# One NeuronCore, adaLN + S4 convolution + squared-ReLU FFN: the first inverse stage in two 64-column tiles, and a re-planned order of the instructions

## The chip, the cores and the metric

The kernel runs on one core of a Trainium2 chip. The metric is the device time of one execution in microseconds (us); lower is better. Each kernel is timed several times, and one further execution is taken with the hardware profiler; all rows of the profile are of that one execution.

## The reference

Input `A_u` has 2048 positions of 512 channels, all float32.

```python
sa, ca, ga, sb, cb, gb = six rows of silu(c) @ w_mod
h = layernorm(x) * (1 + ca) + sa
x = x + ga * ssm_conv(h)              # per channel
h = layernorm(x) * (1 + cb) + sb
x = x + gb * (relu(h @ w1 + b1) ** 2 @ w2 + b2)
# ssm_conv: K[d, l] = Re sum_n C[d,n] dB[d,n] exp(dt A[d,n] l)   (128 states n)
#           y = causal convolution of h with K along l (FFTs of length 4096 in the reference) + h * Dskip
```

The result has the shape of the input.

## The kernel before

**Convolution.** The 512 channels are cut into 8 chunks of 64 (`NC`), and each chunk into 4 units of 16 channels, 32 units in all. The convolution is done with a Fourier transform written as matmuls. For each chunk these pieces exist on PE:

- kernel generation, one per unit ("K", `kgen_mm`, L751): 32 matmuls of 32-column tiles that sum the 128 states into the convolution kernel of 16 channels, in the PSUM bank `kg`;
- stage 1 (`stage1`, L615): 8 matmuls per piece, 64-column stationary tiles; 4 pieces for the input `u` and 4 for the kernel, copied out by ACT (L617);
- stage 2 (`stage2`, L625): 16 matmuls per piece, 64-column tiles, again 4 pieces for each of the two; the result of `u` is copied by ACT (L650) and, once complete, swapped half for half into a second buffer by a DMA on the SP queue (L654); the result of the kernel is multiplied on DVE (L761) with `u` and its swapped copy;
- first inverse stage ("E", L769): 4 pieces of 8 matmuls with 128-column stationary tiles, copied out by ACT (L773).

**What feeds K.** For each chunk POOL makes phase tables with nine integer additions (L684) and scales the amplitudes (L706), and ACT makes 24 exponentials (L703). For each unit POOL adds up the phases (L712, 128x1024) and makes three products of amplitudes (L734, 128x512, two or three named `rtl` and one `rtl` or `llph`); ACT takes sine, absolute value and cosine (L721 to L723); DVE multiplies them together (L740 to L744). The products live in rings of three, so POOL can be three units ahead of K. Once, at the start, `parameters` derives what the tables need from the inputs, on DVE, ACT and POOL (L443 to L493): first for chunk 0 alone, later for chunks 1 to 7 together (128x448 elements, written 7x64). `scale` normalizes the input of a chunk with three DVE instructions of 128x1024 (L603 to L605) and one on POOL (L606).

**After the convolution** the second inverse stage (`inverse`, L937, 32x32 tiles) adds up the result, and the FFN follows (L1031 to L1034 and L1051 to L1053), with its weights split into two parts by ACT (L887, L883) and POOL (L908, L884).

**The order of the work.** Python writes the pieces down in one sequence: `background` gives each chunk's `u` pieces and product pieces a place (`u0` to `u1`, counted in units) between the units. This sequence settles which buffers of the rings a piece uses. Then `keep_order` decides the order on each engine: it walks through all instructions with a price for each (`weight`), starts on the engine that is free first, and picks among the ready instructions the one with the longest priced path to the end, plus a bonus in ns from `urgent` (set by `hurry`). Every engine then executes that list strictly in order. DVE instructions that share a memory port with POOL (`shares_port`) get an extra price.

Of the kernel before, what the change touches and what calls it, by code (L numbers as in the profile page):

```python
# [36 lines left out]
NC = 512 // NCH  # L37
# [58 lines left out]
def weight(ins):  # L96
# [3 lines left out]
    if "DMA" in type(ins).__name__:  # L100
# [12 lines left out]
            tiles = 128 // cols if cols in (32, 64, 128) else 1  # L113
            t = 2.2 * max(moving / 1.2 / tiles + 2, {128: 112, 64: 28}.get(cols, 13))
            return t, t + 170
        case "Activation":
            t = 75 + 0.87 * n + (40 if n > 512 else 0)
            if n == 1:
                t = 200
# [6 lines left out]
            if n <= 4:  # L126
                t = 200
        case "Pool":
            t = 110 + 1.8 * n
        case _:  # L130
# [4 lines left out]
def keep_order(tc, traced, slots, in_turn, whole, urgent):  # L135
# [85 lines left out]
    for g, n in enumerate(left):  # L221
        if n == 0:
            ready[of[g][0]].append(g)
    landed = table = 0
    WINDOW = 3413
# [9 lines left out]
    for _ in groups:  # L235
# [6 lines left out]
        cost = takes[g][0]  # L242
        if e == "PE":
            cost /= level(now)
            a = now
            while a < now + cost - 1:
# [3 lines left out]
                a = b  # L250
        elif e == "DVE" and shares_port(groups[g][0]):
            cost += min(650, max(0, free["Pool"] - now))
        elif e == "Activation":
            new = function_table(groups[g][0]) or table
            cost += 1283 if new != table else 0
            table = new
# [20 lines left out]
def tile_adaln_ssm_ffn(  # L277
# [244 lines left out]
    for i, t in enumerate((mean, rstd)):  # L522
        nc.vector.tensor_copy(t.rearrange("p (s g) -> p s g", g=4), moved[:, :, :, i])
    hurry(mark, 60000)

    for _ in parameters(1, NC - 1):
        pass

# [8 lines left out]
    def mod_rows(wm, ps):  # L537
        for q in range(4):
            for kc in range(4):
                nc.tensor.matmul(  # L540
# [214 lines left out]
    def product_pieces(c):  # L755
# [9 lines left out]
        for g in range(4):  # L765
            ps = bank("ps", PS)
            for i in range(4):
                for h, y in ((0, yu), (1, yr)):
                    nc.tensor.matmul(  # L769
                        ps[:, 128 * i : 128 * i + 128], pairs(y)[:, g, i // 2, :, i % 2],  # L770
                        e1_sb[:, h], start=(h == 0), stop=(h == 1))
            for r in range(2):
# [21 lines left out]
    def background():  # L794

        parts = [(late, 4, 5, 1)]
        for c in range(NC):
            u0 = max(4 * c, 3.9) + (2 if c == 1 else 0)
            parts.append((lambda c=c: u_pieces(c), u0, u0 + (2 if c < 2 else 2.6), 9))
        for c in range(NC - 1):  # L800
            u0 = 4 * c + (4 if c > 0 else 6)
            parts.append((lambda c=c: product_pieces(c), u0, u0 + (2.5 if c == 0 else 3), 8))
        todo = sorted(
# [321 lines left out]
```

## Time and profile before

| what | value |
|---|---|
| median of 3 runs | 712.5 us (709.61 to 714.19) |
| the profiled execution itself | 709.58 us |
| span shown in its profile | 707.8 us |
| PE busy | 596.5 us, 84% of the span |
| DVE, ACT, POOL busy | 392.0, 380.0, 345.3 us |
| first K, unit 0 | starts at 63.05 us |
| last K, unit 31 | starts at 332.05 us |
| second inverse stage | starts at 357.47 us |

Times in rows of the profile are from the start of the span. A row of the timeline gives start, length, engine, line, operation, output<-input, shape and count, and in brackets how long the engine stood idle before and what ended that. PE is the matmuls, PEld the loads of stationary tiles. One float32 matmul of the program leaves two records on PE, so a piece of stage 1 (8 matmuls) is "x16", a piece of stage 2 or a K "x32" or "x64". Lengths of PE rows overlap by some 0.1 us; the price of a piece is best read from one start to the next.

### The profile page before, as it was taken

The page shows a single profiled execution, that of the slowest core. Times are in us where ns is not written, and L with a number is a line of the kernel's source. Part 1 is how long each engine was busy: PE and PEld are TensorE (multiplying, and loading weights), DVE is VectorE, ACT ScalarE, POOL GpSimd, SP SyncE. Part 2 cuts the span into 40 slices and gives each one's busy share as a digit, 9 for nine tenths or more (in the row PEclk, how much of TensorE's full clock was granted, in tenths as well). Part 3 has the DMA queues.
Part 4 walks back from the last instruction along what each step waited for, and adds up shares of the span by engine and source line. Part 5 has one row for each costly group of instructions (what it writes and reads, how often), then busy time and mean ns, then how long its engine had stood idle before and what let it go on. Part 6 is the DMA issues. An engine that isn't in the chain of part 4 may idle for free.

```text
span 707.8 us, 18955 instructions
## 1 busy us (share of the span) xinstructions
PE 596.5 (84%) x8306; PEld 516.4 (73%) x8306; DVE 392.0 (55%) x622; ACT 380.0 (54%) x760; POOL 345.3 (49%) x316
## 2 busy tenths in 40 slices
PE   1321695766989999999868999999999999999996
PEld 1311584765989889999846788888888888888884
DVE  5788889975677576861245784243332533252233
ACT  3464867555999999875626464223432334222220
POOL 5768999999798798740969571000100000000000
PEclk9855798888999999999977999999999999999998
DMA  9990002020202022353822220001000100010001
GB/s 328 374 362 10 3 2 63 1 61 2 63 4 63 18 48 62 106 132 82 288 89 63 77 74 1 1 0 60 0 1 1 60 1 1 0 46 15 1 1 59
DMA packets 22274, 46.38 MB, mean 66 GB/s; under 512 B 3760, under 2 KB 9264, under 8 KB 20400
## 3 DMA queue, kind: packets, MB, share of 16 engines
q1 hardware_dynamic: 21760, 45.04, 20.4%
q8 instruction: 65, 1.06, 0.6%
q10 hardware_dynamic: 432, 0.14, 0.1%
q14 instruction: 17, 0.14, 0.1%
HBM read 32.58 MB, written 4.19 MB: 52 GB/s over the span
## 4 chain that ended last, share of the span: by engine, by line
PE 63%; POOL 20%; DMA 5%; DVE 5%; ACT 5%; issue 3%; DVEq 0%; SPq 0%; POOLq 0%; ACTq 0%
PE tg L1051 7%; PE tg L1053 7%; PE tg L1052 7%; PE ps L769 6%; PE ps L1031 6%; PE ps L1032 6%; PE ps L1034 5%; POOL rtl L734 5%; POOL tables L684 5%; PE ps L625 5%; POOL llph L712 4%; PE ps L615 3%; PE tg L937 2%; PE kg L751 2%; DMA xy<-xt 2%
## 5 line engine op out<-in xcount | busy, mean ns | idle before, releaser
L1039 DVE TENSOR_TENSOR xy<-xy 128x512 f32<-128x512 f32 x56 | 43.9, 784 | 158.9 <-ACT rw L1038 107.6
L1037 ACT ACTIVATE xy<-ps,b1c 128x512 f32<-128x512 f32 x42 | 29.0, 690 | 130.7 <-PE ps L1034 130.7
L966 POOL TENSOR_TENSOR big<-big,b2g 128x512 f32<-128x512 f32 x16 | 21.1, 1318 | 157.7 <-DVE xy L964 153.4
L734 POOL TENSOR_TENSOR rtl<-tables 128x512 f32<-128x512 f32 x75 | 83.9, 1142 | 8.7 <-issue 5.7
L625 PE MATMUL ps<-xy,t_sb 128*64 128x64 f32 x2048 | 71.0, 228 | 10.8 <-DVE xy L761 6.6
L769 PE MATMUL ps<-e_sb,xy 128*128 128x128 f32 x512 | 70.9, 296 | 8.4 <-ACT big L773 5.5
L625 PEld LDWEIGHTS ps<-xy,t_sb 128*64 128x64 f32 x2048 | 67.0, 143 | 14.1 <-DVE xy L761 6.9
L769 PEld LDWEIGHTS ps<-e_sb,xy 128*128 128x128 f32 x512 | 65.5, 204 | 12.0 <-ACT big L773 5.9
L712 POOL TENSOR_TENSOR llph<-tables 128x1024 int32<-128x1024 int32 x32 | 65.1, 2034 | 15.5 <-ACT tg L723 15.3
L617 ACT COPY xy<-ps 128x512 f32<-128x512 f32 x64 | 36.7, 590 | 18.9 <-PE ps L615 18.4
L743 DVE TENSOR_TENSOR rtl<-rtl,tg 128x1024 f32<-128x1024 f32 x32 | 38.9, 1217 | 14.2 <-ACT tg L723 13.4
L721 ACT ACTIVATE tg<-llph 128x1024 f32<-128x1024 int32 x32 | 33.1, 1034 | 25.0 <-POOL llph L712 20.4
L761 DVE TENSOR_TENSOR xy<-ps,xy 128x512 f32<-128x512 f32 x64 | 39.7, 681 | 7.1 <-DMA xy<-xy 6.3
L615 PE MATMUL ps<-d_sb,ksb 128*64 128x128 f32 x512 | 34.2, 281 | 7.1 <-ACT xy L617 4.2
L773 ACT COPY big<-ps 128x256 f32<-128x256 f32 x64 | 33.9, 626 | 10.4 <-PE ps L769 10.4
L615 PE MATMUL ps<-d_sb,big 128*64 128x128 f32 x512 | 33.7, 280 | 5.2 <-DVE xy L761 4.5
L723 ACT ACTIVATE tg<-llph,halfpi 128x1024 f32<-128x1024 f32 x32 | 36.0, 1126 | 1.5 <-DVE llph L744 0.9
L1031 PE MATMUL ps<-h0h,w1h 128*128 128x512 f32 x88 | 36.1, 410 | 0.0
L740 DVE SCALAR_TENSOR_TENSOR rtl<-rtl,tg 128x512 f32<-128x512 f32 x32 | 21.8, 681 | 25.4 <-ACT tg L721 12.4
L540 PE MATMUL ps<-xy,srep 128*32 128x128 f32 x192 | 19.7, 353 | 18.9 <-DMA xy<-w_mod 13.6
L615 PEld LDWEIGHTS ps<-d_sb,ksb 128*64 128x64 f32 x512 | 28.5, 140 | 9.3 <-ACT xy L617 4.7
L722 ACT ACTIVATE llph<-llph 128x1024 f32<-128x1024 int32 x32 | 34.0, 1062 | 0.3
(236 smaller groups left out, 1546.5 us busy)
## 6 DMA issues: line engine op xcount, KB each, us to landing
xy<-xt SPq DMA_DIRECT2D x32, 256.0 KB, 5.4
xy<-xy SPq DMA_DIRECT2D x16, 512.0 KB, 5.9
xy<-w_mod SPq DMA_DIRECT2D x6, 1024.0 KB, 12.4
big<-x SPq DMA_DIRECT2D x4, 1024.0 KB, 11.9
out_dram<-xy SPq DMA_DIRECT2D x16, 256.0 KB, 2.1
xy<-w SPq DMA_DIRECT2D x14, 256.0 KB, 2.8
raw<-w SPq DMA_DIRECT2D x6, 512.0 KB, 5.5
t_sb<-c_t SPq DMA_DIRECT2D x1, 2048.0 KB, 17.1
```

The costliest lines, as they stand in the source:

```text
L615: nc.tensor.matmul(ps[64 * r : 64 * r + 64, 128 * i : 128 * i + 128], src[:, i], d1_sb[:, r], start=True, stop=True)
L625: nc.tensor.matmul(ps[64 * r : 64 * r + 64, 64 * i : 64 * i + 64].rearrange("p (h q t) -> p q h t", h=2, t=2), t2_sb[:, 8 * g + i, r], src ...
L712: nc.gpsimd.tensor_tensor(ph.rearrange("p d r (a b) -> p (d r) a b", a=4), bc(lo[:, us].rearrange("p d r b -> p (d r) b"), 2, 4), bc(hi[:, ...
L734: nc.gpsimd.tensor_mul(o.rearrange("p d (a b) -> p d a b", a=4), bc(p, 3, 8), bc(q, 2, 4))
L761: nc.vector.tensor_mul(product_piece(y, g), ps, piece(x, g))
L769: nc.tensor.matmul(ps[:, 128 * i : 128 * i + 128], pairs(y)[:, g, i // 2, :, i % 2], e1_sb[:, h], start=(h == 0), stop=(h == 1))
L1031: pe.append(nc.tensor.matmul(ps, w1h[:, q, fs], hh[:, q, :], start=(q == 0), stop=False))
L1032: pe.append(nc.tensor.matmul(ps, wl[:, q], hh[:, q, :], start=False, stop=False))
L1039: nc.vector.tensor_mul(rr, rr, rr)
L1051: pe.append(nc.tensor.matmul(acc, r2l[:, ms], hi_, start=(t == 0), stop=False))
L1052: pe.append(nc.tensor.matmul(acc, r2h[:, ms], lo_, start=False, stop=False))
L1053: pe.append(nc.tensor.matmul(acc, r2h[:, ms], hi_, start=False, stop=(t == NF - 1)))
```

## The change

It has three parts.

**E in two tiles.** Each matmul of the first inverse stage, which had a stationary tile of 128 columns, becomes two with 64 columns each that write the two halves of the output partitions. 256 matmuls become 512; the moving operand is the same for both.

**Prices of the planner.** In `weight` the prices of PE shapes, of the reciprocal, of very small DVE instructions and of POOL are replaced; `keep_order` adds 100 ns where PE's shape changes and treats the shared port of DVE and POOL in both directions. No instruction is added or left out by this; only the order moves.

**Places.** The pieces of the chunks get places from two tables. The parameters of chunks 1 to 7 get the bonus of 60000 ns that the statistics of the first layer norm (L508 to L524) had, and these get none. In `mod_rows` the loops are exchanged, so that neighbouring matmuls go to different 32-column tiles.

```diff
-            t = 2.2 * max(moving / 1.2 / tiles + 2, {128: 112, 64: 28}.get(cols, 13))
+            t = max(1.7 * moving / tiles, 60 / tiles)
...
             if n <= 4:
-                t = 200
+                t = 150
+            elif type(ins).__name__ == "InstReciprocal":
+                t = 70 + 6.3 * n
         case "Pool":
-            t = 110 + 1.8 * n
+            t = 180 + 1.72 * n
...
+            kind = free_size(groups[g][0].ins[1]) if len(groups[g][0].ins) > 1 else shape
+            cost += 100 if kind != shape else 0
+            shape = kind
...
-        elif e == "DVE" and shares_port(groups[g][0]):
-            cost += min(650, max(0, free["Pool"] - now))
+        elif e == "DVE":
+            port = shares_port(groups[g][0])
+            cost += min(700, max(0, free["Pool"] - now)) if port else 0
+        elif e == "Pool":
+            cost += min(250, max(0, free["DVE"] - now)) if port else 0
...
-    hurry(mark, 60000)
-
-    for _ in parameters(1, NC - 1):
-        pass
+    hurry(mark, 0)
+
+    for c, n in ((1, 7),):
+        mark = len(nc.cur_bb.bb.instructions)
+        for _ in parameters(c, n):
+            pass
+        hurry(mark, 60000)
...
-        for q in range(4):
-            for kc in range(4):
+        for kc in range(4):
+            for q in range(4):
...
-                    nc.tensor.matmul(
-                        ps[:, 128 * i : 128 * i + 128], pairs(y)[:, g, i // 2, :, i % 2],
-                        e1_sb[:, h], start=(h == 0), stop=(h == 1))
+                    for m in range(2):
+                        nc.tensor.matmul(
+                            ps[64 * m : 64 * m + 64, 128 * i : 128 * i + 128],
+                            pairs(y)[:, g, i // 2, 64 * m : 64 * m + 64, i % 2],
+                            e1_sb[:, h], start=(h == 0), stop=(h == 1))
...
-        parts = [(late, 4, 5, 1)]
-        for c in range(NC):
-            u0 = max(4 * c, 3.9) + (2 if c == 1 else 0)
-            parts.append((lambda c=c: u_pieces(c), u0, u0 + (2 if c < 2 else 2.6), 9))
-        for c in range(NC - 1):
-            u0 = 4 * c + (4 if c > 0 else 6)
-            parts.append((lambda c=c: product_pieces(c), u0, u0 + (2.5 if c == 0 else 3), 8))
+        parts = [(late, 6.00, 8.00, 1)]
+        forward = ((3.30, 4.90), (6.65, 8.75), (8.65, 10.85), (12.65, 14.85), (18.65, 18.85), (22.65, 22.85), (25.15, 26.35), (27.90, 30.10))
+        back = ((6.00, 8.50), (9.00, 12.25), (13.25, 16.25), (16.50, 19.00), (20.75, 24.75), (24.50, 28.00), (28.75, 30.90))
+        for c, (u0, u1) in enumerate(forward):
+            parts.append((lambda c=c: u_pieces(c), u0, u1, 9))
+        for c, (u0, u1) in enumerate(back):
+            parts.append((lambda c=c: product_pieces(c), u0, u1, 8))
```

**What moves.** The rows below are the lists of single engines in the program; `tables_381` are the tables of the even chunks, `tables_382` those of the odd ones, `big_82` holds the parameters, `big_83` the input. Lines of the changed program are 9 to 14 higher: L448 becomes L457, L487 L496, L606 L618, L684 L696, L712 L724, L734 L746, L773 L787, L883 L897.

The first place is the start of POOL's list, after the parameters of chunk 0 (L448 to L453 on 64 elements). Before:

```order
L734 TENSOR_TENSOR rtl<-tables_381 128x16x32 x6
L487 TENSOR_TENSOR big_82<-big_82 128x64 x8
...
L706 TENSOR_TENSOR tables_381<-tables_381,big_82 128x64x4
L712 TENSOR_TENSOR llph<-tables_381 128x1024
L734 TENSOR_TENSOR rtl<-tables_381 128x512
L734 TENSOR_TENSOR llph<-tables_381 128x512 x2
L448 TENSOR_TENSOR big_82<-big_82 128x7x64
...
L453 TENSOR_TENSOR big_82<-big_82 128x7x64
L487 TENSOR_TENSOR big_82<-big_82 128x7x64 x6
L712 TENSOR_TENSOR llph<-tables_381 128x1024
```

Now:

```order
L457 TENSOR_TENSOR big_82<-big_82 128x7x64
...
L462 TENSOR_TENSOR big_82<-big_82 128x7x64
L496 TENSOR_TENSOR big_82<-big_82 128x64
L746 TENSOR_TENSOR rtl<-tables_381 128x16x32 x3
L496 TENSOR_TENSOR big_82<-big_82 128x64 x7
...
L724 TENSOR_TENSOR llph<-tables_381 128x1024
L496 TENSOR_TENSOR big_82<-big_82 128x7x64
L718 TENSOR_TENSOR tables_381<-tables_381,big_82 128x64x4
L724 TENSOR_TENSOR llph<-tables_381 128x1024
L496 TENSOR_TENSOR big_82<-big_82 128x7x64 x7
L746 TENSOR_TENSOR rtl<-tables_381 128x512
```

The parameters of chunks 1 to 7 stand ahead of the products of unit 0 and no longer behind those of units 0 to 2.

The second place is POOL's list just ahead of the last products of unit 11 (the last unit of chunk 2, even tables). Before, from the end of the tables of chunk 3 on:

```order
L606 TENSOR_TENSOR big_83<-big_83,s_319 128x1024
L712 TENSOR_TENSOR llph<-tables_381 128x1024
...
L684 TENSOR_TENSOR tables_381<-big_82,tables_381 128x128
L684 TENSOR_TENSOR tables_381<-big_82 128x128 x2
L684 TENSOR_TENSOR tables_381<-tables_381 128x128x2
L712 TENSOR_TENSOR llph<-tables_382 128x1024
...
L684 TENSOR_TENSOR tables_381<-tables_381 128x128 x3
L606 TENSOR_TENSOR big_83<-big_83,s_319 128x1024
L712 TENSOR_TENSOR llph<-tables_382 128x1024
L734 TENSOR_TENSOR rtl<-tables_381 128x16x32 x2
L734 TENSOR_TENSOR llph<-tables_381 128x512
```

Now:

```order
L724 TENSOR_TENSOR llph<-tables_381 128x1024
L696 TENSOR_TENSOR tables_382<-tables_382 128x128
L746 TENSOR_TENSOR llph<-tables_381 128x512
L696 TENSOR_TENSOR tables_382<-tables_382 128x128x4
L746 TENSOR_TENSOR rtl<-tables_381 128x16x32
L696 TENSOR_TENSOR tables_382<-tables_382 128x128 x2
L746 TENSOR_TENSOR rtl<-tables_381 128x16x32
L696 TENSOR_TENSOR tables_382<-tables_382 128x128
L724 TENSOR_TENSOR llph<-tables_382 128x1024
L746 TENSOR_TENSOR llph<-tables_381 128x512
```

The tables of chunk 4 (again `tables_381`) and the scaling of later chunks stood ahead of unit 11; now only the tables of chunk 3 do, in between the products of units 10 and 11. Counted over the whole list, ahead of the end of unit 11 there stood 45 instructions of L684, 14 of L712 and 5 of L606; now there stand 36, 13 and 3. Up to the end of the last unit both lists hold the same instructions.

The third place is ACT's list at the end of the convolution, where the last four E pieces (chunk 7) are copied out. Before:

```order
L883 CAST w_4657<-xy_91 128x512 x2
L773 COPY big_82<-ps_150 128x4x64
...
L773 COPY big_83<-ps_149 128x4x64
L883 CAST w_4657<-xy_91 128x512
L773 COPY big_82<-ps_150 128x4x64
L773 COPY big_83<-ps_150 128x4x64
```

Now:

```order
L897 CAST w_4913<-xy_91 128x512 x2
L787 COPY big_82<-ps_150 128x4x64
...
L787 COPY big_83<-ps_149 128x4x64
L787 COPY big_82<-ps_150 128x4x64
L787 COPY big_83<-ps_150 128x4x64
L897 CAST w_4913<-xy_91 128x512
```

The third weight split (L883), which reads a freshly loaded part of `w2`, stood ahead of the last two copies and now stands behind them.

On PE the number of pieces between unit 11's K and unit 31's K is, before: 40 of stage 1, 40 of stage 2, 20 of E and 20 K; now: 40 of stage 1, 43 of stage 2, 23 of E and 20 K. Ahead of unit 11's K there stood 7 E pieces, 22 of stage 1 and 20 of stage 2; now there stand 4, 22 and 17. Behind the last K both lists are alike up to the tile size: one E piece, two of stage 1, four of stage 2 and the last four E pieces.

More of the change, by code (lines that the diff above doesn't have):

```diff
@@ L223, in keep_order @@
             ready[of[g][0]].append(g)
-    landed = table = 0
+    landed = table = shape = 0
+    port = False
     WINDOW = 3413
```

## The prediction, as it was recorded before the changed kernel ran

> **What bounds the kernel now.** I read the chain of waits first. Its shares by engine are
>
> ```profile
> PE 63%; POOL 20%; DMA 5%; DVE 5%; ACT 5%; issue 3%; DVEq 0%; SPq 0%; POOLq 0%; ACTq 0%
> ```
>
> so two engines take turns. Where the turn changes is seen from busy times by stage (columns: stretch, its length, busy time of PE, PE's loads, DVE, ACT, POOL, granted clock, DMA share, GB/s):
>
> ```profile
> 62.00:180.00 118.00, 80.64 (x1802) 73.84 (x1804) 93.60 (x113) 76.10 (x163) 116.08 (x99) 0.80 0.09 20
> 186.76:332.05 145.29, 140.43 (x3521) 131.98 (x3521) 95.81 (x152) 129.30 (x254) 105.36 (x104) 1.00 0.27 67
> 400.00:707.80 307.80, 300.93 (x1350) 248.74 (x1349) 121.58 (x177) 100.96 (x179) 32.18 (x23) 0.99 0.06 19
> ```
>
> From 62 to 180 us POOL is busy 116 of 118 us, and PE 81 at a clock of 0.80: POOL sets the pace. From 187 to 332 us PE is busy 140 of 145, and POOL has 40 us to spare. From 400 us on the FFN fills PE, and the change leaves its order alone. So the time is settled by when the last K (unit 31) is reached, and by the passage from there to 400 us.
>
> The timeline gives four Ks on PE (units 0, 7, 11, 31) and, on POOL, the last product of the last three of these:
>
> ```profile
> 63.05 1.95 PE L751 MATMUL kg<-rtl 128*32 128x64 f32 x64 [21.51 <-POOL big L487]
> 120.99 1.95 PE L751 MATMUL kg<-rtl,llph 128*32 128x64 f32 x64 [3.47 <-DVE ksb L825]
> 186.76 1.12 PE L751 MATMUL kg<-rtl,llph 128*32 128x64 f32 x64
> 332.05 1.12 PE L751 MATMUL kg<-rtl,llph 128*32 128x64 f32 x64
> ```
>
> ```profile
> 110.66 1.07 POOL L734 TENSOR_TENSOR llph<-tables 128x512 f32<-128x512 f32 x1
> 167.23 1.06 POOL L734 TENSOR_TENSOR llph<-tables 128x512 f32<-128x512 f32 x1
> 312.18 1.07 POOL L734 TENSOR_TENSOR llph<-tables 128x512 f32<-128x512 f32 x1
> ```
>
> Units 8 to 11 take 65.8 us on PE (120.99 to 186.76). The 20 units after them take 145.3, 29.1 for each chunk of four. Chunk 2 is thus 37 us slower than the later ones, because POOL ends unit 11 only at 168.3. In that time it did work that nothing needed yet (the order of before in the second place). Once ahead, it waited for others. The loss is one of order, not of work.
>
> **The change part by part: POOL up to unit 11.** Early on POOL waits for the parameters of chunks 1 to 7:
>
> ```profile
> 53.60 0.93 POOL L487 TENSOR_TENSOR big<-big 128x448 int32<-128x448 int32 x1 [7.02 <-DVE big L458]
> 56.78 6.29 POOL L487 TENSOR_TENSOR big<-big 128x448 int32<-128x448 int32 x5 [2.24 <-DVE big L476]
> ```
>
> Now these stand first, and between their DVE steps POOL has chunk 0's tables to do: 7.02 + 2.24 = 9.3 us of idle time go. Unit 0's last product comes later for it, but its K started only at 63.05 us for other reasons, so I give that no cost; uncovered it would cost up to the 9.3 us back.
>
> Then 9 instructions of L684 (a set of tables), one of L712 and two of L606 no longer stand ahead of unit 11. Their prices, from a stretch without crowding (the four L684 rows make one set):
>
> ```profile
> 226.02 0.54 POOL L684 TENSOR_TENSOR tables<-big,tables 128x128 int32<-128x128 int32 x1
> 226.51 0.47 POOL L684 TENSOR_TENSOR tables<-big 128x128 int32<-128x128 int32 x1
> 261.41 0.40 POOL L684 TENSOR_TENSOR tables<-big 128x128 int32<-128x128 int32 x1
> 261.88 3.63 POOL L684 TENSOR_TENSOR tables<-tables 128x256 int32<-128x256 int32 x6
> 250.46 1.95 POOL L712 TENSOR_TENSOR llph<-tables 128x1024 int32<-128x1024 int32 x1
> 171.44 1.90 POOL L606 TENSOR_TENSOR big<-big,s 128x1024 f32<-128x1024 f32 x1
> ```
>
> 5.04 + 1.95 + 2 x 1.90 = 10.8 us. They are not saved, only done later, where POOL had 40 us to spare.
>
> Third, DVE and POOL slow each other while DVE scales an input chunk. One of its three instructions per chunk shows it (min/median/max in ns):
>
> ```profile
> L603 DVE TENSOR_TENSOR big<-big,mean x8: 1214/2147/2966, 42.3 to 149.1; 128x1024 f32<-128x1024 f32 x8
> ```
>
> Median less minimum is 0.93 us. What POOL loses by each the rows do not show; it lies between nothing and the 1.75 us from minimum to maximum, and I take 0.93. All 24 such instructions stood ahead of unit 11 on DVE's list, now 17 do: 7 x 0.93 = 6.5 us (0 to 12).
>
> Unit 11 ends on POOL at 168.3 - 9.3 - 10.8 - 6.5 = 141.7 us. K followed its last product by 9.3 us at unit 7 and by 18.5 at unit 11, where PE had three more E pieces to do first. I take 8: the K of unit 11 at **150 us**, 37 us earlier.
>
> **PE from unit 11 to unit 31.** Prices from one start to the next:
>
> ```profile
> 212.58 2.08 PE L625 MATMUL ps<-xy,t_sb 128*64 128x64 f32 x64
> 214.59 2.15 PE L769 MATMUL ps<-e_sb,xy 128*128 128x128 f32 x16
> 216.67 1.12 PE L751 MATMUL kg<-rtl 128*32 128x64 f32 x64
> 217.73 2.15 PE L769 MATMUL ps<-e_sb,xy 128*128 128x128 f32 x16
> 219.81 1.97 PE L615 MATMUL ps<-d_sb,ksb 128*64 128x128 f32 x32
> 221.71 1.25 PE L751 MATMUL kg<-rtl,llph 128*32 128x64 f32 x64
> ```
>
> Stage 2 costs 2.01 / 2 = 1.0 us, E 2.08, K 1.06, stage 1 1.90 / 2 = 0.95. Before: 40 x 0.95 + 40 x 1.0 + 20 x 2.08 + 20 x 1.06 = 141 us of work in 145.3, 3% more than the work.
>
> An E piece in 64-column tiles is not in the trace. Two pieces of stage 1 have the same 16 matmuls of 64 columns by 128, alternating between the halves: 1.90 us. Different stationary tiles over one moving operand, as E will have, are in stage 2, and there the tiles overlap too. The other end is no overlap, 3.8 us (a rival below). I take 1.90, saving 0.18 for each of 32 pieces. The Trainium skill, TensorEngine Tiling (Array Packing), section Key Properties, says that a change of tiling mode drains TensorE. By it the drains on both sides of E go as well; the rows above show no gap over 0.1 us at such a change, so it would be worth a few us at most.
>
> Now: 38 + 43 x 1.0 + 23 x 1.90 + 21.2 = 146 us of work. POOL has in the same stretch 60 x 1.06 + 19 x 1.95 + 4 x 5.04 + 5 x 1.90, some 130 us, plus 6.5 of crowding, and ACT 129 as before. All lie below PE, but POOL no longer runs ahead, so PE will wait now and then. What these waits cost lies between 3%, as now with POOL ahead, and 118 / 80.6 = 46%, as in 62 to 180 us. I take 8%, near the lower end, because between two Ks PE's list holds pieces of earlier chunks that need nothing from POOL. 146 x 1.08 = 158 us: the last K at 150 + 158 = **308 us**, 24.5 earlier than now (307.5 unrounded).
>
> **The passage to the second inverse.** Rows of before, in time:
>
> ```profile
> 332.78 3.07 SPq L654 DMA_DIRECT2D xy<-xy  x2
> 340.13 4.88 DVE L761 TENSOR_TENSOR xy<-ps,xy 128x512 f32<-128x512 f32 x8 [6.31 <-DMA xy<-xy]
> 356.26 0.62 ACT L883 CAST w<-xy 128x512 fp32r<-128x512 f32 x1 [2.66 <-DMA xy<-w]
> 356.79 1.02 ACT L773 COPY big<-ps 128x256 f32<-128x256 f32 x2
> 357.47 3.69 PE L937 MATMUL tg<-big,i2c 32*32 32x128 f32 x219 [3.07 <-POOL w1lb L908]
> ```
>
> The last two E copies stand behind a weight split that waits 2.66 us for a DMA; now they stand ahead of it. The swap of chunk 7 was issued after the last K; now stage 2 of its input is done ahead of the K of unit 30, which is worth up to 0.8 us. Four E pieces give 4 x 0.18 = 0.7. Sum 4.2 at best, nothing if the last row is right that POOL's L908 released PE; I take **3.5**, since the copy at 356.79 ends its first half just ahead of PE's start.
>
> The exchanged loops of the modulation shorten PE work that lies under POOL's stage: no cost or gain. The new prices cost nothing on the chip by themselves.
>
> **The sum.** The span of 707.8 us and 1.8 us around it make the 709.6 us of the profiled execution. 709.6 - 24.5 - 3.5 = 681.6 us. The median lies 2.9 us above that execution, so I forecast 684.5.
>
> **The rivals.**
> *Most of it is given back (20%).* Three fixed lists run close to full, and each error in one stops the others. For it speaks that POOL's surplus of 40 us shrinks to about 10; against it that PE's list is mixed. With 20% of waits the last K comes at 150 + 175 = 325: 702 us.
> *No change (8%).* The gain on POOL does not reach PE: chunk 0's delay costs the 9.3 us, crowding moves along to later chunks, and waits reach 25%. The last K is at 332 again, 709 to 712 us.
> *Slower (8%): PE starves and its clock falls.* After a wait, pieces of before took nearly double:
>
> ```profile
> 153.09 3.78 PE L769 MATMUL ps<-e_sb,xy 128*128 128x128 f32 x16 [5.55 <-ACT big L773]
> 168.21 3.64 PE L625 MATMUL ps<-xy,t_sb 128*64 128x64 f32 x64 [6.59 <-DVE xy L761]
> ```
>
> If PE has such waits through the second half, 146 us of work take 35% more, 197: the last K at 347, 724 us. It decides above 25%, that is, when a chunk of four units takes over 36 us. Against it: in 187 to 332 us the clock was 1.00 throughout. The Trainium skill, TensorE: Matmul & The Clock Gate, Part 1, names the mechanism: after an idle window of some 3.4 us the clock is halved. The two rows, with waits of 5.5 and 6.6 us, agree.
> *Slower (4%): the E tiles do not overlap.* 1.9 us more on 23 + 4 pieces is 51 us over the forecast: 736 us. Stage 2's rows speak against it.
>
> **How the numbers follow.** My forecast has 60%; with lags of 5 to 10 us, waits of 3 to 15% and the bounds above its own range is 671 to 700. The range of 668 to 706 adds a larger gain on POOL and the first rival. A measurement of this kernel can tell about 1% (7 us) from no change. Faster by over 1%: 60 + 20 = 80%; within it 8%; slower 12%.
>
> **What would show it.** Right: POOL busy without a gap over 3 us up to unit 11, whose K starts at 142 to 158 us; chunks of 30 to 33 us after it; E pieces at 1.9 us from start to start; the last K at 298 to 318; the second inverse 22 us after it (25.4 before); the FFN's length unchanged. Wrong: K of unit 11 after 165 us, chunks over 36 us, or a clock below 0.95 between the two Ks.

## The result and the profile after

The changed kernel takes 678.56 us (median of 4 runs, 674.74 to 680.01), the kernel before 711.75 (4 runs on the same chip, 709.61 to 714.19): a ratio of 0.9524, with a 95% interval from 0.9473 to 0.9576. Forecast were 684.5 us in a range from 668 to 706. The profiled execution is the fastest of the four: 674.74 us, a span of 673.0, against the 681.6 of the sum.

Busy times by stage, after (columns as in the prediction: stretch, its length, busy time of PE, its loads, DVE, ACT, POOL, granted clock, DMA share, GB/s):

```profile
62.00:180.00 118.00, 99.73 (x2684) 91.82 (x2686) 105.53 (x144) 102.67 (x222) 116.67 (x98) 0.96 0.17 39
147.71:303.23 155.52, 143.87 (x4036) 136.79 (x4033) 111.68 (x171) 138.52 (x267) 131.92 (x124) 0.99 0.27 66
365.00:673.00 308.00, 301.12 (x1351) 248.87 (x1349) 122.51 (x177) 101.35 (x179) 33.14 (x23) 0.99 0.06 19
```

The first row answers to the 62 to 180 us of before: POOL is as busy as it was (116.67 against 116.08), but PE does 99.7 us of work beside it instead of 80.6, at a clock of 0.96 instead of 0.80. The last row shows the FFN unchanged (308.0 against 307.8 us).

The K of unit 11 and of unit 31 on PE, and the last product of units 11 and 31 on POOL:

```profile
139.19 2.05 POOL L746 TENSOR_TENSOR llph<-tables 128x512 f32<-128x512 f32 x1
147.71 1.12 PE L763 MATMUL kg<-rtl,llph 128*32 128x64 f32 x64
288.26 1.07 POOL L746 TENSOR_TENSOR llph<-tables 128x512 f32<-128x512 f32 x1
303.23 1.12 PE L763 MATMUL kg<-rtl,llph 128*32 128x64 f32 x64
```

Unit 11 ends on POOL at 141.2 us (168.3 before), its K comes at 147.7 (186.8), the last K at 303.2 (332.1). The second inverse starts at 325.94 instead of 357.47. So the span's 34.8 us are 28.8 up to the last K, 2.7 in the passage and 3.3 behind it.

POOL's part can be split with two rows of busy times, before and after, from 13 us (where it has its first data) to its last product of unit 11. Columns: stretch, length, POOL busy, clock, DMA share, GB/s.

```profile
13.00:168.29 155.29, 140.20 (x128) 0.77 0.33 112
```

```profile
13.00:141.24 128.24, 124.38 (x115) 0.97 0.41 136
```

POOL's idle time went from 15.1 to 3.9 us, its work from 140.2 to 124.4. By the prediction's prices 10.8 of these 15.8 us are work that is now done later, and 5.0 are crowding. POOL's rows show the crowding itself: in each kernel 24 of them are 0.7 to 1.1 us longer than the shortest row of the same form, one beside each of DVE's 24 scaling instructions. All 24 lie ahead of unit 11's end in the kernel before, 16 in the changed one.

### The profile page after: what moved, and what is told of

It reads as the page before. It is cut to its first block, busy times and chain, and to the rows that moved or that the text cites. A ratio compares the mean times of both kernels' runs of the same rounds, so it can differ in the third digit from the quotient of the medians.

```text
span 673.0 us, 19998 instructions
## 1 busy us (share of the span) xinstructions
PE 573.0 (85%) x8818; PEld 497.2 (74%) x8818; DVE 392.2 (58%) x622; ACT 379.1 (56%) x759; POOL 349.8 (52%) x316
## 4 chain that ended last, share of the span: by engine, by line
PE 55%; POOL 22%; ACT 8%; DVE 6%; issue 5%; DMA 3%; DVEq 0%; SPq 0%; POOLq 0%; ACTq 0%
PE tg L1065 8%; PE tg L1066 7%; PE tg L1067 7%; POOL rtl L746 6%; PE ps L1045 6%; PE ps L1046 6%; PE ps L1048 6%; POOL llph L724 5%; POOL tables L696 4%; PE ps L637 4%; PE ps L782 2%; POOL llph L746 2%; PE kg L1045 2%; PE kg L1046 2%; PE kg L1048 2%
## 5 line engine op out<-in xcount | busy, mean ns | idle before, releaser
L1053 DVE TENSOR_TENSOR xy<-xy 128x512 f32<-128x512 f32 x56 | 41.8, 746 | 156.5 <-ACT rw L1052 105.6
L980 POOL TENSOR_TENSOR big<-big,b2g 128x512 f32<-128x512 f32 x16 | 21.7, 1356 | 154.0 <-DVE xy L978 152.7
L746 POOL TENSOR_TENSOR rtl<-tables 128x512 f32<-128x512 f32 x75 | 92.3, 1243 | 8.2 <-PE kg L763 8.0
L637 PEld LDWEIGHTS ps<-xy,t_sb 128*64 128x64 f32 x2048 | 68.0, 145 | 13.1 <-DVE xy L773 6.0
L724 POOL TENSOR_TENSOR llph<-tables 128x1024 int32<-128x1024 int32 x32 | 66.9, 2090 | 0.7 <-ACT tg L735 0.3
L782 PE MATMUL ps<-e_sb,xy 128*64 128x128 f32 x1024 | 62.4, 279 | 4.9 <-DVE xy L773 2.2
L782 PEld LDWEIGHTS ps<-e_sb,xy 128*64 128x64 f32 x1024 | 57.7, 142 | 6.6 <-DVE xy L773 2.6
L773 DVE TENSOR_TENSOR xy<-ps,xy 128x512 f32<-128x512 f32 x64 | 40.1, 682 | 8.9 <-ACT ksb L902 6.4
L733 ACT ACTIVATE tg<-llph 128x1024 f32<-128x1024 int32 x32 | 33.2, 1037 | 15.5 <-DVE rtl L754 11.2
L787 ACT COPY big<-ps 128x256 f32<-128x256 f32 x64 | 34.9, 626 | 10.3 <-PE ps L782 10.0
L763 PE MATMUL kg<-rtl 128*32 128x64 f32 x704 | 13.2, 229 | 25.4 <-DVE rtl L756 25.4
L734 ACT ACTIVATE llph<-llph 128x1024 f32<-128x1024 int32 x32 | 34.2, 1070 | 0.4
L696 POOL TENSOR_TENSOR tables<-tables 128x128 int32<-128x128 int32 (+2 forms) x48 | 31.9, 670 | 1.6
```

What stands on the lines that cost most here:

```text
L637: nc.tensor.matmul(ps[64 * r : 64 * r + 64, 64 * i : 64 * i + 64].rearrange("p (h q t) -> p q h t", h=2, t=2), t2_sb[:, 8 * g + i, r], src ...
L696: iadd = lambda o, p, q: nc.gpsimd.tensor_tensor(o, p, q, op=ALU.add)
L724: nc.gpsimd.tensor_tensor(ph.rearrange("p d r (a b) -> p (d r) a b", a=4), bc(lo[:, us].rearrange("p d r b -> p (d r) b"), 2, 4), bc(hi[:, ...
L746: nc.gpsimd.tensor_mul(o.rearrange("p d (a b) -> p d a b", a=4), bc(p, 3, 8), bc(q, 2, 4))
L782: nc.tensor.matmul(ps[64 * m : 64 * m + 64, 128 * i : 128 * i + 128], pairs(y)[:, g, i // 2, 64 * m : 64 * m + 64, i % 2], e1_sb[:, h], st ...
```

## The experiments

The first theory, **A**, is that of the prediction: the amount of work on POOL ahead of unit 11's last product sets the K of unit 11, and PE's work sets what follows. Four kernels undid one part of the change each. "Ratio" is always to the kernel before, timed on the same chip (709.0 to 709.4 us there); "cost" is the ratio less the change's 0.9524, in us of 709. The change's own interval is 3.7 us to each side, so a cost of 2 or 3 us is not told from none.

**E in one 128-column tile again** (`e1_wide`), with every list in the order of the changed kernel:

```diff
-                    for m in range(2):
-                        nc.tensor.matmul(
-                            ps[64 * m : 64 * m + 64, 128 * i : 128 * i + 128],
-                            pairs(y)[:, g, i // 2, 64 * m : 64 * m + 64, i % 2],
-                            e1_sb[:, h], start=(h == 0), stop=(h == 1))
+                    nc.tensor.matmul(
+                        ps[:, 128 * i : 128 * i + 128], pairs(y)[:, g, i // 2, :, i % 2],
+                        e1_sb[:, h], start=(h == 0), stop=(h == 1))
```

> The changed kernel with the first inverse stage (E) back in one 128-column tile; the planner is told the same price, so every engine keeps the changed kernel's order. Theory (POOL sets unit 11's K, PE sets what follows): K of unit 11 stays at 147.7 us within 2; the 23 E pieces between it and unit 31 cost 0.31 to 0.33 us more each, so the last K comes 7.5 us later, at 311, and four more pieces add 1.3 us in the passage: 687 us. Rival (the cheaper E fell into PE's waits, 11.7 us between those two Ks): the last K stays within 3 us of 303, 679 to 682 us.

Measured: 678.48 us, ratio 0.9569 (0.9528 to 0.9611), a cost of 3 us that is not told from none. An E piece takes 2.09 us from start to start in one tile and 1.75 in two, as the rows show, first of this kernel and then of the changed one:

```profile
111.88 2.15 PE L781 MATMUL ps<-e_sb,xy 128*128 128x128 f32 x16
113.97 1.97 PE L627 MATMUL ps<-d_sb,big 128*64 128x128 f32 x32
```

```profile
111.83 1.92 PE L782 MATMUL ps<-e_sb,xy 128*64 128x128 f32 x32
113.58 1.92 PE L627 MATMUL ps<-d_sb,big 128*64 128x128 f32 x32
```

The K of unit 11 stays (147.63), the last K comes 3.9 us later (307.15), where 23 x 0.34 = 7.8 us more work went into that stretch. So theory A failed here: half of what the tiles save on PE falls into waits for other engines before the last K. The second inverse starts only 2.0 us later (327.99), but that is no second such loss: the last four E pieces took 7.80 us here and 8.88 in the changed kernel, whose clock fell to half behind the same wait of 2.23 us (see the passage, below).

**Parameters late again** (`e3_params_late`):

```diff
-    hurry(mark, 0)
-    for c, n in ((1, 7),):
-        mark = len(nc.cur_bb.bb.instructions)
-        for _ in parameters(c, n):
-            pass
-        hurry(mark, 60000)
+    hurry(mark, 60000)
+    for _ in parameters(1, NC - 1):
+        pass
```

> The changed kernel with the statistics urgent again and the parameters of chunks 1 to 7 behind them, as before the change; prices, places and tiles stay. Theory: POOL's two idle times (9.3 us) come back ahead of unit 11 and nothing makes them up: unit 11's last product ends at 150 us, its K at 157, the last K at 310 to 312, 687 us. Rival (what POOL loses early PE makes up later, since its list is mixed): K of unit 11 later, but the last K within 3 us of 303, 678 to 681 us.

Measured: 695.72 us, ratio 0.9796 (0.9764 to 0.9828): a cost of 19 us, twice what the theory gave and far above the rival. The idle time came back as forecast, and more beside it:

```profile
53.69 1.10 POOL L496 TENSOR_TENSOR big<-big 128x448 int32<-128x448 int32 x1 [6.74 <-DVE big L467]
56.81 7.55 POOL L496 TENSOR_TENSOR big<-big 128x448 int32<-128x448 int32 x6 [2.02 <-DVE big L485]
63.54 0.68 DVE L756 TENSOR_TENSOR rtl<-rtl,tg 128x512 f32<-128x512 f32 x1
64.36 1.95 PE L763 MATMUL kg<-rtl 128*32 128x64 f32 x64 [25.23 <-POOL big L496]
156.12 1.07 POOL L746 TENSOR_TENSOR llph<-tables 128x512 f32<-128x512 f32 x1
162.59 1.12 PE L763 MATMUL kg<-rtl,llph 128*32 128x64 f32 x64 [0.33 <-DVE ksb L839]
```

6.74 + 2.02 = 8.8 us of idle time, but unit 11 ends on POOL at 157.2, 16 us later than in the changed kernel: from 13 us on POOL is idle for 14.0 us instead of 3.9, and its 115 instructions, as many as there, take 130.2 us instead of 124.4. The first K also comes 11.8 us later (64.36 against 52.57). The row names POOL as its releaser, but K reads what DVE makes, and DVE ends unit 0's last factor at 64.2 us, since steps of the late parameters stand ahead of it on its list. From unit 11 to unit 31 the new order takes 5.5 us longer, too (last K at 323.56).

**The planner's old prices** (`e4_old_prices`): `weight` and `keep_order` as before the change, all else as after.

```diff
-            t = max(1.7 * moving / tiles, 60 / tiles)
+            t = 2.2 * max(moving / 1.2 / tiles + 2, {128: 112, 64: 28}.get(cols, 13))
...
-            t = 180 + 1.72 * n
+            t = 110 + 1.8 * n
...
-        elif e == "Pool":
-            cost += min(250, max(0, free["DVE"] - now)) if port else 0
...
```

> The changed kernel with the planner's old prices; the tiles, the early parameters and the new places stay. On POOL's list 9 instructions of table building, 2 scales and one phase sum stand ahead of unit 11's last product again, 11.7 us by their rows, and all of DVE's input scaling. Theory: that product ends at 153 to 159 us instead of 141 (the higher figure with 6.5 us of crowding), its K at 160 to 166; PE has by then done 9 us of pieces more and has POOL ahead of it again, so the rest takes 140 to 146 us and the last K comes at 303 to 310: 679 to 686 us. Rival 1 (a delay on POOL before unit 11 is passed on in full): the last K at 315 to 321, 690 to 697 us. Rival 2 (POOL's order had no part in the gain): K of unit 11 stays at 148, 678 us.

Measured: 707.38 us, ratio 0.9976 (0.9957 to 0.9995): a cost of 32 us, so nearly the whole gain is gone. POOL behaves as theory A said, PE does not (lines of this kernel: L715 is the phase sum, L724 the sine, L778 the copy of E):

```profile
137.00 1.03 ACT L724 ACTIVATE tg<-llph 128x1024 f32<-128x1024 int32 x1 [3.96 <-POOL llph L715]
139.07 3.68 PE L773 MATMUL ps<-e_sb,xy 128*64 128x128 f32 x32 [4.08 <-ACT big L778]
144.27 1.12 PE L754 MATMUL kg<-rtl,llph 128*32 128x64 f32 x64
153.54 1.06 POOL L737 TENSOR_TENSOR llph<-tables 128x512 f32<-128x512 f32 x1
179.25 1.12 PE L754 MATMUL kg<-rtl,llph 128*32 128x64 f32 x64
```

Unit 11's product ends at 154.6, inside the 153 to 159 forecast. But its K comes at 179.25, 25 us behind it (6.5 in the changed kernel), and the last K at 333.56. The K of unit 8 stands at 144.27, although DVE had finished that unit's factors some 20 us earlier. It was held up by the E piece ahead of it on PE's list, that by copies on ACT, and those by a sine at the head of ACT's list that waited for POOL's phase sum.

**The old places** (`e5_old_places`):

```diff
-        forward = ((3.30, 4.90), (6.65, 8.75), ...)
-        back = ((6.00, 8.50), (9.00, 12.25), ...)
+        for c in range(NC):
+            u0 = max(4 * c, 3.9) + (2 if c == 1 else 0)
+            parts.append((lambda c=c: u_pieces(c), u0, u0 + (2 if c < 2 else 2.6), 9))
...
```

> The changed kernel with the old places of the chunks' pieces in the program; prices, early parameters and tiles stay. POOL has 3.6 us less ahead of unit 11 than in the changed kernel, PE three pieces of stage 2 and two of E more (6.5 us). Theory: the places do little by themselves once the prices are right: unit 11's last product ends at 138 us, its K comes at 146 to 150, the last K within 4 us of 303: 675 to 683 us. Rival (the gain came from the places, which keep the lists level in the second half): chunks of more than 33 us behind unit 11, the last K at 315 or later, 690 us and more.

Measured: 685.53 us, ratio 0.9659 (0.9627 to 0.9692), a cost of 10 us, between the two. Unit 11's product ends at 139.2 us, 2 us earlier than in the changed kernel, yet its K comes at 155.53 and the last at 312.37. Again POOL is early and K late, but not because PE waits: in the 16.3 us between the two PE is busy for 15.3, with pieces that stand ahead of the K on its list.

**Theory B** came from the rows of `e4_old_prices`: it is not the amount on POOL that counts but what stands in line. An instruction at the head of ACT's or DVE's list that waits for POOL holds up copies and products behind it, PE waits for those, and the Ks that have long been ready stand behind PE's waiting piece. The kernel before shows both cases (its waits on PE, at 153.09 and 168.21, are in the prediction):

```profile
138.21 1.51 POOL L684 TENSOR_TENSOR tables<-big,tables 128x128 int32<-128x128 int32 x1
148.07 2.93 POOL L712 TENSOR_TENSOR llph<-tables 128x1024 int32<-128x1024 int32 x1
151.03 1.03 ACT L721 ACTIVATE tg<-llph 128x1024 f32<-128x1024 int32 x1 [5.70 <-POOL llph L712]
152.00 1.04 ACT L773 COPY big<-ps 128x256 f32<-128x256 f32 x2
158.42 1.12 PE L751 MATMUL kg<-rtl,llph 128*32 128x64 f32 x64
166.28 0.69 DVE L740 SCALAR_TENSOR_TENSOR rtl<-rtl,tg 128x512 f32<-128x512 f32 x1 [5.83 <-POOL rtl L734]
166.88 2.48 DVE L761 TENSOR_TENSOR xy<-ps,xy 128x512 f32<-128x512 f32 x4
```

From 138 us POOL builds the tables of chunk 3 and only then forms unit 11's phase sum (148.07). ACT's sine waits 5.70 us for it, with E's copies behind it; PE's E piece waits 5.55 us for them, with the K of unit 8 behind it. At 166.28 DVE waits in the same way for unit 11's product. Two kernels move only POOL's instructions and keep every other list as it was.

**One phase sum earlier** (`p_a`), the kernel before with the order that the planner found and one move in it:

```diff
+    lo, hi = place[pool["table"][27]], place[pool["phase"][11]]
+    behind(pool["phase"][11], [g for g in turns[lo:hi] if of[g][0] == "Pool"])
```

Here `turns` is the planned order of all instructions; `behind(g, late)` takes those in `late` out of it and puts them right after `g`. Table 27 is the first of chunk 3.

> The kernel before with its order kept on every engine but for one instruction: on POOL the phase sum of unit 11 (it started at 148.07 us) goes ahead of the tables of chunk 3 and one scale (10 us of work that began at 138.21). What POOL has ahead of unit 11's last product stays the same. Theory A (the amount of work ahead of that product decides): it ends at 168.3 us as before, the K of unit 11 at 187, 709 to 712 us. Theory B (POOL holds PE through ACT's queue: ACT's sine of unit 11 waited 5.70 us for this phase sum with E's copies queued behind it, and PE waited 5.55 us for those with the K of unit 8 queued behind): the sine starts at 146 to 147 instead of 151.0, PE's wait shrinks to under 2 us, the K of unit 8 comes at 153 to 155 instead of 158.4; the K of unit 11 gains 0 to 3 us, since the next tables on POOL's list are still ahead of unit 11's products; 707 to 711 us.

Measured: 710.54 us, ratio 1.0009 (0.9994 to 1.0025): no change, as both theories allowed, and the trace tells them apart:

```profile
146.47 1.04 ACT L721 ACTIVATE tg<-llph 128x1024 f32<-128x1024 int32 x1
152.14 1.12 PE L751 MATMUL kg<-rtl,llph 128*32 128x64 f32 x64
166.07 0.69 DVE L740 SCALAR_TENSOR_TENSOR rtl<-rtl,tg 128x512 f32<-128x512 f32 x1 [10.36 <-POOL rtl L734]
168.01 3.68 PE L625 MATMUL ps<-xy,t_sb 128*64 128x64 f32 x64 [11.16 <-DVE xy L761]
```

The sine's wait is gone, the K of unit 8 comes 6.3 us earlier, and all of it is waited away at the next place in line: DVE now waits 10.36 us for unit 11's product instead of 5.83, PE 11.16 instead of 6.59.

**The products earlier too** (`p_ab`):

```diff
+    lo, hi = place[pool["table"][36]], place[pool["product"][33]]
+    behind(pool["product"][35], [g for g in turns[lo:hi] if of[g][0] == "Pool"])
```

> As the run before, and the three products of unit 11 on POOL also go ahead of the tables of chunk 4, two phase sums and a scale (15 us). All else keeps the order of the kernel before. Theory A: the last product ends at 153 us, the K of unit 11 follows after 9 to 18 us, at 162 to 171, and the gain of 16 us or more is passed on: 690 to 697 us. Theory B: the products use a buffer that the K of unit 8 must have read, so POOL waits for that K (153 to 155 us) and ends at 158; the K of unit 11 comes at 175 to 180, the last K 7 to 10 us earlier, 700 to 704 us.

Measured: 703.85 us, ratio 0.9907 (0.9886 to 0.9928).

```profile
153.19 3.40 POOL L734 TENSOR_TENSOR rtl<-tables 128x512 f32<-128x512 f32 x2 [1.88 <-PE kg L751]
156.54 1.07 POOL L734 TENSOR_TENSOR llph<-tables 128x512 f32<-128x512 f32 x1
176.57 1.12 PE L751 MATMUL kg<-rtl,llph 128*32 128x64 f32 x64
```

POOL now waits for PE: unit 11's factors go into the buffer that the K of unit 8 must have read, there being three. The product ends at 157.6 and the K of unit 11 comes at 176.57, as theory B said (158; 175 to 180); theory A said 153 and 162 to 171. So part of what POOL was busy with in the kernel before was work taken up because the next product could not start yet: the K of unit 8 ended there at 159.5 us, and unit 11's first product began at 165.17.

What fills the time from POOL's product to the K of unit 11 (the lag) is mostly PE's own pieces, which stand ahead of that K on its list (us; the clock is the one granted in that time):

| kernel | product's end | K of unit 11 | lag | PE busy in it | clock |
|---|---|---|---|---|---|
| before | 168.3 | 186.76 | 18.5 | 18.5 | 0.91 |
| changed | 141.2 | 147.71 | 6.5 | 4.5 | 0.74 |
| `e4_old_prices` | 154.6 | 179.25 | 24.7 | 18.5 | 0.73 |
| `e5_old_places` | 139.2 | 155.53 | 16.3 | 15.3 | 1.00 |
| `p_ab` | 157.6 | 176.57 | 19.0 | 17.4 | 1.00 |

Of the 10.2 us at unit 11, 4.5 are left at the last K (327.58), less than the 7 to 10 forecast, and 0.93% or 6.6 us in the time, inside theory B's 700 to 704.

**E in two tiles alone** (`e2_split_only`): the kernel before with the new lines of E and the order kept.

> The kernel before with E in two 64-column tiles, its order kept on every engine by telling the planner the old price. Theory A (from unit 11 on PE's work sets the time): 20 E pieces at 0.33 us less and 4 in the passage, 8 us less: 702 to 704 us. Theory B (it falls into waits for other engines, as 4 of the 9 us did under the new order): 3 to 4 us less, 706 to 708 us.

Measured: 708.33 us, ratio 0.9974 (0.9953 to 0.9994): 2 us, just short of B's 3 to 4, and about what undoing it cost.

**The modulation's loops exchanged back** (`e6_mod_old`):

```diff
-        for kc in range(4):
-            for q in range(4):
+        for q in range(4):
+            for kc in range(4):
```

> The changed kernel with the modulation's two loops exchanged back, its order kept on every engine. Six sets of 16 matmuls take 2.7 instead of 1.0 us each at full clock, 10 us more of PE work, all ahead of unit 8. Theory (it lies under the wait for other engines): within 2 us of the changed kernel, 677 to 681 us. Rival (PE is near its limit there too, between units 0 and 8): 4 to 8 us more, 683 to 687 us.

Measured: 678.59 us, ratio 0.9548 (0.9529 to 0.9568), not told apart from the changed kernel's 0.9524. PE spends 16.6 us on the six sets instead of 9.7 (group rows, count, busy time and mean in ns; first this kernel, then the changed one), all of it under other waits.

```profile
L552 PE MATMUL ps<-xy,srep 128*32 128x128 f32 x192 | 16.6, 316 | 14.5 <-DVE big L484 14.5
```

```profile
L552 PE MATMUL ps<-xy,srep 128*32 128x128 f32 x192 | 9.7, 371 | 15.1 <-DMA xy<-w_mod 15.1
```

**Each planning part alone.** If undoing one part loses up to 32 of 34 us, the parts can't simply add up. Three kernels put one part each into the kernel before; their diffs are those of `e4`, `e3` and `e5` read the other way.

> The kernel before with the planner's new prices alone; parameters late, old places, E in one tile. POOL has 15 us less ahead of unit 11's last product (12 table instructions, 2 scales and 2 phase sums go behind it), but keeps the 9.3 us of waiting for parameters. If the parts work only together (what one frees on POOL, the others must not fill or wait away): the product ends at 150 to 154 us, the K of unit 11 at 160 to 168, 690 to 700 us. If each part keeps the share that it lost when it alone was undone in the changed kernel (32 us for the prices): 677 to 680 us.

Measured: 693.50 us, ratio 0.9768 (0.9743 to 0.9793). Unit 11's product ends at 152.7 us, its K comes at 168.23, the last K at 320.25: inside the first set of figures but for the K of unit 11, which lies at its upper edge.

> The kernel before with the parameters of chunks 1 to 7 ahead of the statistics, nothing else. POOL no longer waits for them, but under the old prices the planner fills the time: 45 table instructions and 6 scales still stand ahead of unit 11's last product. If the parts work only together: the K of unit 11 within 8 us of 187 and 702 to 712 us. If the part keeps the share that it lost when undone alone (20 us): 687 to 692 us.

Measured: 699.97 us, ratio 0.9864 (0.9837 to 0.9891), 2 us below the first set of figures and 8 above the second. Unit 11's product ends at 158.1, its K comes at 177.54 (9.2 us earlier than before, where 8 were allowed), the last K at 325.08.

> The kernel before with the new places of the chunks' pieces alone. POOL has 5.6 us less ahead of unit 11's last product (3 table instructions, one scale, one phase sum). If the parts work only together: the K of unit 11 at 180 to 187, the old prices still set tables ahead, 703 to 713 us. If the part keeps the share that it lost when undone alone (10 us): 697 to 701 us.

Measured: 719.05 us, ratio 1.0137 (1.0117 to 1.0158): slower than before, and above both forecasts. The K of unit 11 comes at 186.94, as before, but the last K at 345.88 (332.05 before). Between the two PE has the same pieces as before but one, yet it stands idle for 14.9 us of that stretch instead of 4.9, nearly all of it ahead of unit 27, and more pieces are left for the last chunk, which takes 40.1 us instead of 30.1. Under the old prices the new places leave nine pieces of stage 1, twelve of stage 2 and seven of E between the Ks of units 27 and 31, where it was eight, eight and five: 9 x 0.95 + 12 x 1.0 + 7 x 2.08 = 35 us instead of 26, besides the Ks, and PE has no slack there (length, then PE's busy time, of most of that chunk):

```profile
309.50:345.90 36.40, 35.35 (x766) 33.45 (x762) 12.94 (x22) 21.21 (x38) 5.64 (x6) 1.00 0.46 117
```

| part | alone in the kernel before | undone in the changed kernel |
|---|---|---|
| prices | -16 us (0.9768) | +32 us (0.9976) |
| parameters first | -10 us (0.9864) | +19 us (0.9796) |
| places | +10 us (1.0137) | +10 us (0.9659) |
| E in two tiles | -2 us (0.9974) | +3 us (0.9569), not told from none |
| modulation | not tried | +2 us (0.9548), not told from none |
| all together | -34 us (0.9524) | |

Alone, the parts that were tried make 18 us; together they make 34. The places are a loss in the kernel before and a gain in the changed one. The two moves on POOL's list made 6.6 us; which other moves of the new order make the rest is not shown.

**Four products earlier on DVE** (`q_dve`), the changed kernel with one move that theory B asks for:

```diff
+    behind(d[i + 4], [d[i - 1], d[i]])
```

`d` is DVE's list, `d[i]` the instruction of unit 11 that waits for POOL's product, `d[i - 1]` the scaling step ahead of it, `d[i + 4]` the fourth of the products behind it.

> The changed kernel with one move on DVE and the order kept everywhere else: four products with a spectrum, which wait at 138 us behind a scaling step and behind an instruction of unit 11 that itself waits for POOL's product (it ends at 141.2), go ahead of those two. Theory B (an instruction at the head of DVE's queue that waits for POOL holds the products behind it, and PE waits for those): PE's wait of 4.18 us at 143.2 falls under 2 us, the K of unit 11 comes at 144 to 146 instead of 147.7, and as much of that as PE's later waits don't take reaches the end: 1 to 3 us, 675.5 to 677.5 us. Theory A (K follows POOL's product): K and time stay, 678 to 679 us.

Measured: 678.09 us, ratio 0.9560 (0.9534 to 0.9585): no gain. The K of unit 11 comes at 145.27 as forecast, but the next ones late in line take it back:

```profile
145.27 1.12 PE L763 MATMUL kg<-rtl,llph 128*32 128x64 f32 x64
167.46 1.46 PE L627 MATMUL ps<-d_sb,big 128*64 128x128 f32 x16 [2.22 <-DVE xy L773]
168.70 1.93 PE L637 MATMUL ps<-xy,t_sb 128*64 128x64 f32 x32
181.04 1.40 PE L627 MATMUL ps<-d_sb,ksb 128*64 128x128 f32 x16 [2.91 <-DVE ksb L839]
182.22 3.33 PE L782 MATMUL ps<-e_sb,xy 128*64 128x128 f32 x32
```

At 167.46 PE has waited 2.22 us for DVE (L773), and goes on when the changed kernel does (167.52): the 2.4 us gained are gone there. Behind that wait the clock is 0.51 (168 to 170 us), and a piece of stage 2 takes 1.86 us from start to start instead of 1.03. At 181.04 PE waits again, 2.91 us, and the E piece after it takes 3.33 us instead of 1.97. Unit 15's K is 4.1 us later than in the changed kernel (186.41), the last K 3.4 (306.61).

## Why the prediction was right, and where not

**POOL up to unit 11: right.** 9.3 us of idle time, 10.8 of work put off and 6.5 of crowding were to bring its end to 141.7 us. Measured are 11.2 of idle time and 15.8 of work and crowding, and 141.2. How the 15.8 divide rests on the prediction's own prices; that 8 of the 24 lengthened POOL rows, by some 1 us each, moved behind unit 11 speaks for its 6.5 us rather than for the 5.0 that the subtraction leaves. The term put at nothing, chunk 0's delay, had even the other sign: the first K came at 52.57 us instead of 63.05, and `e3_params_late` shows why.

**"POOL sets the pace": half right.** The ends of POOL's units and the Ks do move together, but the link is not the amount of work ahead of a product. `p_a` and `p_ab` show two links: ACT's and DVE's lists, where one instruction that waits for POOL holds up what PE needs, and the buffers, where a product waits for a K. They show too that POOL's 98% in 62 to 180 us held work that was done while a buffer was still in use. The lag of 8 us from POOL's product to the K of unit 11, chosen between 9.3 and 18.5 because of three E pieces, was the step that carried the risk. It came out at 6.5 in the changed kernel, at 25 in `e4_old_prices` and at 16 in `e5_old_places`, with POOL ending within 14 us of the same time. Its reason was of the right kind: what stands ahead of the K on PE's list makes most of the lag (the table under `p_ab`). But three E pieces of 2.1 us cover 6 us, and in `e4_old_prices` the lag grew by 18: PE had 14 us more of pieces, partly at half clock, and 4 us more of waits. That the lag fell near 8 was in part luck.

**PE from unit 11 to unit 31: right in size.** 155.5 us against 158. The 8% of waits was a choice between 3 and 46%, so that it came out is luck; PE was idle for 11.7 of the 155.5 us, 8% of its 143.9 us of work. E cost 1.75 us from start to start instead of 1.90, 23 x 0.15 = 3.4 us less. The chunks took 34.6, 30.7, 34.9, 28.8 and 26.5 us; only one of the five lies in the 30 to 33 forecast. What the forecast did not see is that E's saving hardly matters: `e1_wide` and `e2_split_only` find 2 to 3 us for all of it (the first not told from none), since PE waits a little longer elsewhere.

**The passage: 2.7 us instead of 3.5.** The two steps named happened, but one of them gained nothing:

```profile
311.39 4.88 DVE L773 TENSOR_TENSOR xy<-ps,xy 128x512 f32<-128x512 f32 x8 [6.39 <-ACT ksb L902]
316.33 8.88 PE L782 MATMUL ps<-e_sb,xy 128*64 128x128 f32 x128 [2.23 <-DVE xy L773]
325.25 1.03 ACT L787 COPY big<-ps 128x256 f32<-128x256 f32 x2 [0.70 <-PE ps L782]
326.66 0.62 ACT L897 CAST w<-xy 128x512 fp32r<-128x512 f32 x1 [0.38 <-DMA xy<-w]
```

The products no longer wait for the DMA that swaps chunk 7 (6.31 us before). The 6.39 us in the first row are no such wait: PE starts stage 2 of this chunk only at 310.14, and the products follow its first piece. From the last K to the start of the four E pieces it took 13.1 us, 13.0 before, so the swap's 0.8 us did not show. All of the 2.7 us lie behind: from there to the second inverse it took 9.6 us instead of 12.4, with the last E copies ahead of the weight split.

Chance has a part in it. The granted clock fell to 0.50 (318 to 320 us) after E's wait of 2.23 us, as it had in the kernel before after one of 2.44 (0.59 from 345.06 to 349 us). In `e6_mod_old` the same wait left it at 1.00, the same four pieces took 7.21 us, and the whole passage 21.0 us instead of 22.7:

```profile
319.31 7.21 PE L782 MATMUL ps<-e_sb,xy 128*64 128x128 f32 x128 [2.23 <-DVE xy L773]
```

**Behind the second inverse: 3.3 us that were in no step.** From its start to the end it took 347.1 us, 350.3 before. In the 14 kernels profiled here this stretch takes 347.1 to 351.0 us, with the FFN's order the same, so the 3.3 us are within what it varies by. Together: 4.3 us of the 6.8 by which the profiled execution undercut the sum lie ahead of the last K, 3.3 here, and 0.8 the other way in the passage.

**The rivals.** "Most is given back" needed 20% of waits; it was 8%. "No change" needed chunk 0's delay, and the first K came earlier. PE's clock was 0.99 between the two Ks, so it did not starve. E's tiles do overlap. The rival that was missing is the one `b_places` shows: pieces pushed into the last chunk, where PE is full. In the changed kernel, with the other parts beside the places, it did not come true: its last chunk took 26.5 us.

## What to carry to other kernels

A queue that is busy 98% of the time need not be what sets the pace: look at what it is doing, and whether the next needed instruction could have started, before pricing the time by the sum of its work. When in-order queues feed each other, follow a late instruction back by who stands at the head of each list, and expect a move of one instruction to pass the wait to the next list (6.3 us gained at one K, nothing at the end). Parts of a reordering do not add up (18 us alone, 34 together; one of them 10 us slower alone), so a part should be judged with the others in place.

## What the runs showed of the hardware

- Two 64-column tiles over one moving operand made a piece of 16 matmuls of 128 columns by 128 cheaper, 1.75 us instead of 2.09 from start to start. The 16 matmuls of the modulation, with neighbours now in different 32-column tiles, cost 1.6 us a set instead of 2.8 (9.7 and 16.6 for six, some at half clock), although the mean of one matmul rises from 316 to 371 ns.
- PE's clock fell to half after waits as short as 2.22 and 2.91 us (`q_dve`: clock 0.51 and 0.50, 3.33 us for an E piece of 1.97), but not after every such wait: behind 2.23 us it fell to 0.50 in the changed kernel and stayed at 1.00 in `e6_mod_old`, 8.88 against 7.21 us for the same four pieces. The Trainium skill, TensorE: Matmul & The Clock Gate, Part 1, names an idle window of some 3.4 us; the earlier waits of 5.5 and 6.6 us agree with it, and these are shorter.
- DVE and POOL crowding comes in steps of 1 us on POOL's rows: a product takes 1.06 or 2.05 us, a phase sum 1.95 or 2.94. In both kernels each of DVE's 24 scaling instructions (128x1024) met one POOL row that was 0.7 to 1.1 us longer than the shortest of its form, and no other POOL row exceeded the shortest of its form by more than 0.6 us. With the new order the median of the first scaling step on DVE fell from 2.15 to 1.45 us. Up to unit 11 POOL had 16 such rows instead of 24; the other 8 moved behind it. Its busy time over the whole kernel did not fall but rose, from 345.3 to 349.8 us.
